# Constant matrix products in an attention stage's waits, a transposed layout for gate products, and weight remainders moved from GpSimd to VectorE

## The chip, the core and the metric

The kernel runs on one core of one Trainium2 chip. The metric is the device time of one execution in microseconds. The engines are TensorE (PE, with PEld for its weight loads), VectorE (DVE), ScalarE (ACT), GpSimd (POOL) and SyncE (SP), which here only issues DMAs.

## The reference

A linear attention without softmax feeds a mixture of experts in which each token goes to one expert.

```python
kv = einsum('bhsd,bhse->bhde', k, v)            # 8 batches, 8 heads, 576 tokens, 64 values
out = einsum('bhsd,bhde->bhse', q, kv)
out = out / sqrt(mean(out * out, -1) + 1e-6) * g_norm
x = out.transpose(0, 2, 1, 3).reshape(4608, 512)
e_idx = argmax(x @ w_gate, axis=1)              # 8 experts
gate_w = softmax(x @ w_gate)[token, e_idx]
eom = sigmoid(x @ w_output_gate)
for e in range(8):                              # w1[e]: 512 x 1024, w2[e]: 1024 x 512
    mask = e_idx == e
    y[mask] = gate_w[mask] * eom[mask, e] * (relu(x[mask] @ w1[e]) @ w2[e])
```

## The kernel before

**Attention stage (`p1_main`, to about 118 us).** For each batch, `kv_part` (line 469) multiplies k and v of five chunks of tokens (four of 128 and one of 64) into one PSUM tile, 64 x 64 per head, two heads side by side. `kvT_part` (494) transposes the result with two products against the identity. `m_part` (503) multiplies it by the gate weights (16 values per head: 8 logits and 8 output gates). Both results stand together in `augs`, so that `out_tile` (524) gets, with one product per pair of heads, the attention output of 128 tokens and every head's share of the gate products. The 36 output tiles of a batch are done while the next batch is worked on. ScalarE copies each tile out of PSUM in three steps: the rows (555), their squares (557), the gate products `gp` (558). `gp` has the layout token tile, head, 16 values.

**Routing.** The 36 tiles fall in four groups (10, 10, 4, 12). `route` (581) is a generator that `advance` moves on by a step after each tile. It works out the reciprocal norms (597 to 620, in `xtail`), scales `gp` by them (627; group 0 on GpSimd, the others on VectorE), sums over the heads (631, `lg`), takes the maximum and the expert's one-hot row (`ohb`), counts with products of `ones` (690), and places each token: `la` (717 to 731) is a one-hot matrix per tile, made by GpSimd, ScalarE or VectorE as the letters of `PLACES` say. After group 2 (24 tiles) the largest expert is known: the lead expert. Its first 384 rows are run 0, its other rows run 1 (3 tiles); runs 2 to 8 are the other experts.

**Precision.** Products run in fp32r with each operand split into a high and a low part: three products instead of one. `split` (199) makes the high part of a 128 x 1024 block of weights on one engine and the low part (weights minus high part) on another. `SPLITS` gives the engines for the lead expert: four blocks of first weights, then four of second weights. A `P` as second letter means GpSimd. Rows are scaled by their norms in `scale_heads` (245): on GpSimd ahead of time (`scale_rows`) or, with a `V` in `NORMS`, on VectorE when the tile is staged.

**Order.** In the attention stage the order on TensorE, ScalarE, VectorE and GpSimd is the order of the program, written by hand with `HOOKS` (steps after a given tile) and `TAIL` (steps after the last tile): `L` is the next step of the lead expert (`stage`, `split`, `mm1`), `S` the next split of its second weights, `R` one `advance`. In the expert part it is by hand for TensorE, ScalarE and VectorE. Between the two, a planner puts instructions that are ready into gaps; so the first nine products of `mm2` stand ahead of the sixth `mm1` step. Every engine runs its queue in order. Loads are issued by SyncE as memory slots come free.

**Buffers in PSUM.** `ps_b` (tag "big", 2 tiles) serves the output tiles, `m_part` and `mm1`; `ps_t` (tag "t", 2 tiles) serves `kv_part`, `kvT_part` and the row transposes of `stage`.

Of the kernel before, what the change touches and what calls it, by code (L numbers as in the profile page):

```python
# [11 lines left out]
F32 = mybir.dt.float32  # L12
# [5 lines left out]
ALU = mybir.AluOpType  # L18
AX = mybir.AxisListType
ET = mybir.EngineType  # L20

P = 128
B, H, S, D = 8, 8, 576, 64
NTOK = B * S
DM = H * D
E = 8
# [5 lines left out]
W = D + 2 * E  # L32
# [16 lines left out]
GMAX = max(GR)  # L49
# [28 lines left out]
APART = (2,)  # L78


SPLITS = ['VV', 'AV', 'AV', 'AV', 'AP', 'AP', 'AP', 'AP']
NORMS = ("PPP", "VPVP")
PLACES = ['P', 'P', 'PAV', 'PAV', 'PAV']

ROUND = 1.5 * 2.0 ** 30

# [49 lines left out]
def body(ctx: ExitStack, tc: tile.TileContext, kvm, rem, qT, wg, gn, w1, w2, kc, xs, tab, out):  # L136
    nc = tc.nc
# [27 lines left out]
    ps_t = main.enter_context(tc.tile_pool(name="ps_t", bufs=2, space=psum))  # L165
# [237 lines left out]
    sm = p1.enter_context(tc.tile_pool(name="sm", bufs=2))  # L403
# [7 lines left out]
    w = XW - DM  # L411
# [11 lines left out]
    ones = c1.tile([P, P], BF16, name="ones")  # L423
# [33 lines left out]
    def load(spare):  # L457

        while loads and len(free) > spare:
# [6 lines left out]
            nc.sync.dma_start(out=t[:n], in_=src)  # L466
            where[k] = t

    def kv_part(b):

        r = rt[b // 2]
        q0 = (b % 2) * 64
        ps = ps_t.tile([P, 512], F32, name="kvps", tag="t")
        for s in range(5):
            for p in range(NP):
                for u in range(2):
                    c = slice(p * P + u * D, p * P + (u + 1) * D)
                    if s < 4:
                        k, v = kvt[(b, s)][:, 0, c], kvt[(b, s)][:, 1, c]
                    else:  # L480
                        k, v = r[q0:q0 + 64, 0, c], r[q0:q0 + 64, 1, c]

                    nc.tensor.matmul(ps[u * D:(u + 1) * D, p * D:(p + 1) * D], k, v, start=(s == 0 and p == 0),  # L483
                                     stop=(s == 4 and p == NP - 1))
        for c in range(4):
            give(kvt.pop((b, c)))
        if b % 2:
            give(rt.pop(b // 2))
        nc.scalar.copy(augs[b % 3][:, :, 0:D], ps[:, 0:NP * D].rearrange("q (p d) -> q p d", p=NP))
        cp = wk.tile([P, NP * D], F32, name="kvc", bufs=1)  # L490
        nc.vector.tensor_copy(cp, ps[:, 0:NP * D])
        return cp

    def kvT_part(cp):

        ps = ps_t.tile([P, 2, P], F32, name="kvTps", tag="t")
        for i in range(2):
            nc.tensor.transpose(ps[:, i, :], cp[:, i * P:(i + 1) * P], ident)
        t = wk.tile([P, 2, P], F32, name="kvT", bufs=1)
        nc.scalar.copy(t, ps)  # L500
        return t

    def m_part(b, kvT):
        a = augs[b % 3]
        ps = ps_b.tile([P, 2, 512], F32, name="mps", tag="big")
        for i in range(2):
            for u in range(2):
                for w in range(2):
                    r = slice(w * D, (w + 1) * D)
                    nc.tensor.matmul(ps[u * D:(u + 1) * D, w, i * 16:i * 16 + 16], kvT[r, i, u * D:(u + 1) * D],  # L510
                                     gw[r, i, u * 16:u * 16 + 16], start=True, stop=True)
        nc.scalar.copy(a[:, :, D:D + 16].rearrange("q (i w) x -> q w i x", w=2),
                       ps[:, :, 0:32].rearrange("q w (i x) -> q w i x", i=2))
# [10 lines left out]
    def out_tile(g):  # L524
        gi, t, n = group_of(g)
        if t == 0:
            gst[gi] = (sm.tile([P, GMAX, E], F32, name="ss"),
                       sm.tile([P, GMAX, H, 16], F32, name="gp"),
                       sm.tile([P, GMAX, 16], F32, name="lg"))
        ss, gp, lg = gst[gi]  # L530
        if g in BIG:
            chunk[:] = [g, mem.tile([P, BIG[g], DM], F32, name="xrow", tag=f"xT{list(BIG).index(g)}")]
        elif not chunk:
            chunk[:] = [g, take([P, 2, DM], F32, "xrow")]
        xrow = chunk[1][:, g - chunk[0]]
        ps = ps_b.tile([P, 2, 512], F32, name="ops", tag="big")
        parts = []
        n0 = g * P
        while n0 < (g + 1) * P:
            b = n0 // S  # L540
            n1 = min((g + 1) * P, (b + 1) * S)
            parts.append((b, n0 - g * P, n1 - n0))
            n0 = n1
        for p in range(NP):
            for b, r0, m in parts:
                q0 = g % 2 * P + r0

                for u in range(2):
                    r = slice(u * D, (u + 1) * D)
                    nc.tensor.matmul(ps[r0:r0 + m, u, p * W:(p + 1) * W], qt[g // 2][r, p, q0:q0 + m],  # L550
                                     augs[b % 3][r, p, :], start=True, stop=True)
        if g % 2:
            give(qt.pop(g // 2))
        v = ps[:, :, 0:NP * W].rearrange("q u (p x) -> q u p x", p=NP)
        nc.scalar.copy(xrow.rearrange("q (p u d) -> q u p d", p=NP, u=2), v[:, :, :, 0:D])  # L555
        sq = wk.tile([P, H, D], F32, name="sq", bufs=4)
        nc.scalar.activation(sq.rearrange("q (p u) d -> q u p d", u=2), v[:, :, :, 0:D], AF.Square)  # L557
        nc.scalar.copy(gp[:, t].rearrange("q (p u) x -> q u p x", u=2), v[:, :, :, D:W])  # L558
        squares.append((sq, ss[:, t, :], gi if t + 1 == n else None))
        c0, x = chunk  # L560
        k = x.shape[1]
        if g + 1 == c0 + k:
            xwrite(c0, xs[1 + c0 * P:1 + (c0 + k) * P, 0:DM].rearrange("(t p) x -> p t x", p=P), x)
            chunk.clear()
# [16 lines left out]
    def route(gi):  # L581
# [4 lines left out]
        ss, gp, lg = gst[gi]  # L586
        n = len(GROUPS[gi])
        last = gi + 1 == len(GROUPS)
        g0 = GROUPS[gi][0]
        vec = nc.vector  # L590
# [13 lines left out]
        u = sm.tile([P, GMAX, E], F32, name="ru")[:, :n]  # L604
        rv = xtail[:, g0:g0 + n, C_RMS - DM:C_RMS - DM + H]

        q = 0.375 ** 0.5
# [14 lines left out]
        gpv = gp[:, :n]  # L622
        halves = [slice(0, E), slice(E, 2 * E)] if gi in APART else [slice(0, 2 * E)]

        def scaled(j, eng):
            w = j.stop - j.start
            eng.tensor_tensor(out=gpv[:, :, :, j], in0=gpv[:, :, :, j],
                              in1=rv.unsqueeze(3).to_broadcast([P, n, E, w]), op=ALU.mult)

        def summed(j):  # L630
            vec.tensor_reduce(out=lg[:, :n, j], in_=gpv[:, :, :, j].rearrange("p t h j -> p t j h"), axis=AX.X, op=ALU.add)

        scaled(halves[0], veng(gi))
        if gi in APART:
# [211 lines left out]
    def p1_main():  # L846
        load(SPARE)
        for b in range(B):
            lim = tiles_ready(b - 1) if b else 0
            cp = kv_part(b)  # L850
            load(SPARE)
            run_out(lim)
            kvT = kvT_part(cp)
            run_out(lim)
            run_out(lim)
            m_part(b, kvT)
            while done_tiles < lim:
                run_out(lim)
        while done_tiles < NT:
            run_out(NT)  # L860
        for step in TAIL:
            act(step)
        while routing:
            advance()

    vec = nc.vector
# [315 lines left out]
```

## Time and profile before

| | |
|---|---|
| median of 3 runs (604.76, 607.0, 602.8 us) | 604.76 us |
| the profiled execution's own time | 609.39 us |
| span of the profile | 607.4 us |
| mean granted clock of TensorE | 0.934 |
| TensorE busy | 557.5 us (92%), 4179 products |
| VectorE, ScalarE, GpSimd busy | 262.4, 221.0, 163.4 us |

The span runs from the first to the last instruction; the 2 us beside it are start and end. "Granted clock" is the share of TensorE's full clock of 2.4 GHz that it was given; 0.50 is 1.2 GHz. In the 40 slices of the page the clock is below full in the first ten (some 152 us) and full from there on, apart from the end. TensorE is busy 90% or more of nearly every slice after the eleventh.

### The profile page before, as it was taken

What the parts mean: (1) busy time and instruction counts of PE and PEld (TensorE: products, weight loads), DVE (VectorE), ACT (ScalarE), POOL (GpSimd) and SP (SyncE); (2) the same over time, 40 slices, a digit from 0 to 9 for tenths busy, and PEclk for the clock granted to TensorE, in tenths of its full rate; (3) what the DMA queues carried; (4) which work ended last, traced back from release to release, by engine and by line L of the source; (5) the groups of instructions that cost most, each with busy time, mean ns of one, the idle gap of its engine ahead of it and who ended that gap; (6) DMA issues with size and microseconds to landing.
All of it is one profiled execution on the core that took longest, in us unless ns stands there. A gap on an engine that the chain in (4) does not pass through costs nothing.

```text
span 607.4 us, 10470 instructions
## 1 busy us (share of the span) xinstructions
PE 557.5 (92%) x4179; PEld 497.3 (82%) x4179; DVE 262.4 (43%) x546; ACT 221.0 (36%) x413; POOL 163.4 (27%) x163
## 2 busy tenths in 40 slices
PE   3889879858999999999999999999999999999991
PEld 3678868747788899889988987998799889889880
DVE  1123588789614556415440443235235325424300
ACT  0425564644224435323432343234234423523310
POOL 2001044542860620540063027104500630110010
PEclk9957786578999999999999999999999999999997
DMA  8999993590563622442334333524432452110010
GB/s 271 364 408 409 404 375 85 168 373 2 141 242 122 210 91 73 138 171 72 103 119 155 104 105 98 169 70 141 139 120 70 138 183 71 53 53 2 4 49 10
DMA packets 33459, 92.24 MB, mean 152 GB/s; under 512 B 8801, under 2 KB 8929, under 8 KB 33408
## 3 DMA queue, kind: packets, MB, share of 16 engines
q1 hardware_dynamic: 26672, 71.63, 33.4%
q0 software_dynamic: 6304, 19.70, 10.3%
q8 instruction: 34, 0.56, 0.4%
q10 hardware_dynamic: 432, 0.21, 0.1%
q14 instruction: 17, 0.14, 0.1%
HBM read 72.34 MB, written 19.70 MB: 152 GB/s over the span
## 4 chain that ended last, share of the span: by engine, by line
PE 63%; issue 17%; DMA 7%; DVE 6%; ACT 3%; POOL 2%; SPq 0%; POOLq 0%; DVEq 0%
PE yps L359 26%; PE hps L310 25%; PE ops L550 4%; PE kvps L483 3%; PE tps L272 3%; DMA ld<-rem 2%; DMA ld<-qT 2%; PE yps L353 2%; POOL out L370 2%; DMA ld<-kvm 2%; ACT xrow L555 1%; ACT sq L557 1%; DMA wraw<-w 1%; DMA xg<-xs,gidx 1%; DVE ss L571 1%
## 5 line engine op out<-in xcount | busy, mean ns | idle before, releaser
L310 PE MATMUL hps<-xT,whi 128*128 128x256 f32 (+8 forms) x1024 | 192.3, 306 | 9.2 <-DVE hT L326 8.1
L359 PE MATMUL yps<-whi,hT 128*128 128x512 f32 (+3 forms) x592 | 194.9, 397 | 0.0
L310 PEld LDWEIGHTS hps<-xT,whi 128*128 128x128 f32 x1024 | 159.4, 191 | 11.8 <-DVE hT L326 8.8
L359 PEld LDWEIGHTS yps<-whi,hT 128*128 128x128 f32 (+3 forms) x592 | 110.1, 186 | 24.1
L310 PE MATMUL hps<-xT,wlo 128*128 128x304 f32 (+8 forms) x512 | 119.2, 304 | 0.0
L359 PE MATMUL yps<-wlo,hT 128*128 128x512 f32 (+3 forms) x296 | 115.9, 392 | 0.0
L326 DVE SCALAR_TENSOR_TENSOR hT<-hps,hT 128x512 fp32r<-128x512 f32 (+6 forms) x112 | 57.9, 518 | 124.2 <-ACT hT L325 124.2
L325 ACT ACTIVATE hT<-hps 128x512 fp32r<-128x512 f32 (+6 forms) x112 | 51.6, 461 | 151.8 <-PE hps L310 118.8
L310 PEld LDWEIGHTS hps<-xT,wlo 128*128 128x128 f32 x512 | 87.0, 190 | 0.0
L370 POOL DMA_INDIRECT out<-y,oidx x42 | 44.8, 1068 | 154.2 <-ACT y L369 109.5
L240 POOL DMA_INDIRECT xg<-xs,gidx x42 | 42.4, 1010 | 138.1 <-PE tps L272 92.1
L359 PEld LDWEIGHTS yps<-wlo,hT 128*128 128x128 f32 (+3 forms) x296 | 55.1, 186 | 11.2
L218 DVE SCALAR_TENSOR_TENSOR wlo<-wraw,gcol,whi 128x1024 fp32r<-128x1024 f32 x32 | 44.6, 1394 | 40.3 <-ACT whi L215 40.3
L550 PE MATMUL ops<-aug,ld 64*128 64x80 f32 (+1 forms) x640 | 49.2, 328 | 5.9 <-ACT gp L558 5.6
L248 POOL TENSOR_TENSOR xg<-xg 128x512 f32<-128x512 f32 (+7 forms) x40 | 44.3, 1110 | 31.9 <-DMA xg<-xs,gidx 31.6
L550 PEld LDWEIGHTS ops<-aug,ld 64*128 64x128 f32 (+1 forms) x640 | 44.8, 231 | 8.8 <-ACT gp L558 6.4
L369 ACT ACTIVATE y<-yps,tl 128x512 f32<-128x512 f32 (+3 forms) x37 | 25.5, 689 | 71.7 <-PE yps L359 68.6
L277 ACT CAST xT<-tps 128x512 fp32r<-128x512 f32 (+9 forms) x45 | 23.2, 519 | 68.0 <-PE tps L272 66.2
L483 PE MATMUL kvps<-ld 128*64 128x64 f32 (+1 forms) x640 | 36.4, 298 | 11.8 <-DMA ld<-kvm 10.9
L278 DVE TENSOR_TENSOR xT<-tps,xT 128x512 fp32r<-128x512 f32 (+9 forms) x45 | 27.2, 605 | 45.4 <-ACT xT L277 44.9
L483 PEld LDWEIGHTS kvps<-ld 128*64 128x64 f32 (+1 forms) x640 | 32.9, 207 | 14.9 <-DMA ld<-kvm 12.5
L225 DVE TENSOR_TENSOR wlo<-wraw,whi 128x1024 fp32r<-128x1024 f32 x28 | 34.3, 1225 | 14.1 <-ACT whi L222 8.7
(159 smaller groups left out, 403.7 us busy)
## 6 DMA issues: line engine op xcount, KB each, us to landing
wraw<-w SPq DMA_DIRECT2D x64, 512.0 KB, 3.3
ld<-kvm SPq DMA_DIRECT2D x32, 512.0 KB, 10.2
ld<-qT SPq DMA_DIRECT2D x18, 512.0 KB, 10.2
xs<-xrow SPq DMA_DIRECT2D x13, 512.0 KB, 10.3
xs<-xrow SPq DMA_DIRECT2D x2, 1280.0 KB, 13.7
ld<-rem SPq DMA_DIRECT2D x3, 512.0 KB, 11.0
xg<-xs,gidx POOLq DMA_INDIRECT x42
out<-y,oidx POOLq DMA_INDIRECT x42
```

The source lines that it names most:

```text
L218: eng.scalar_tensor_tensor(out=lo, in0=r, scalar=gcol[:, 0:1], in1=hi.bitcast(F32), op0=ALU.mult, op1=ALU.subtract)
L225: eng.tensor_tensor(out=lo, in0=r, in1=hi.bitcast(F32), op=ALU.subtract)
L240: nc.gpsimd.indirect_dma_start(out=x[:M, :], out_offset=None, in_=rows, in_offset=bass.IndirectOffsetOnAxis(ap=gidx[:M, p, t:t + 1], axis=0))
L248: eng.tensor_tensor(out=v, in0=v, in1=f, op=ALU.mult)
L278: nc.vector.tensor_tensor(out=lo[:, :, c0:c0 + M], in0=v, in1=hi.bitcast(F32)[:, :, c0:c0 + M], op=ALU.subtract)
L310: nc.tensor.matmul(ps[:, j, :n], w[:, o:o + P], x[d][:, j * N:j * N + n], start=(d == 0 and k == 0), stop=(d == 3 and k == 2))
L325: nc.scalar.activation(hh, x, AF.Relu)
L326: nc.vector.scalar_tensor_tensor(out=v(h[:, l:l + n]), in0=x, scalar=0.0, in1=hh.bitcast(F32), op0=ALU.max, op1=ALU.subtract)
L359: nc.tensor.matmul(ps[:M], a, b, start=(f == 0 and k == 0), stop=(f == 7 and k == 2))
L370: i_ = nc.gpsimd.indirect_dma_start(out=out, out_offset=bass.IndirectOffsetOnAxis(ap=oidx[:M, p, t:t + 1], axis=0), in_=y[:M], in_offset=N ...
L483: nc.tensor.matmul(ps[u * D:(u + 1) * D, p * D:(p + 1) * D], k, v, start=(s == 0 and p == 0), stop=(s == 4 and p == NP - 1))
L550: nc.tensor.matmul(ps[r0:r0 + m, u, p * W:(p + 1) * W], qt[g // 2][r, p, q0:q0 + m], augs[b % 3][r, p, :], start=True, stop=True)
```

## The change

Four edits. Constant products: `constant` multiplies the 128 x 128 matrix `ones` (bf16) by a view of itself that is 128, 256 or 512 columns wide; the results are not read. They stand ahead of each kv chunk of 128 tokens in batches 0 to 2, ahead of the transposes in `kvT_part`, ahead of the products of `m_part`, and (512 columns, in a `ps_t` tile of their own) behind them. The gate products `gp` get the heads innermost. The four second weights of the lead expert get their low parts on VectorE instead of GpSimd, and one tile of run 1 is scaled there (`NORMS`; the fourth letter has no tile). In the last group, `la` is made on VectorE where it was on GpSimd (`PLACES`, 4 of 12 tiles).

```diff
-SPLITS = ['VV', 'AV', 'AV', 'AV', 'AP', 'AP', 'AP', 'AP']
-NORMS = ("PPP", "VPVP")
-PLACES = ['P', 'P', 'PAV', 'PAV', 'PAV']
+SPLITS = ['VV', 'AV', 'AV', 'AV', 'AV', 'AV', 'AV', 'AV']
+NORMS = ("PPP", "VVVV")
+PLACES = ['P', 'P', 'PAV', 'VAV']
+COLD_B = 3
+COLD = (2, 20, 2, 3, 3)
...
+    def constant(ps, n, start=True):
+        for _ in range(n):
+            k = ps.shape[1] // P
+            nc.tensor.matmul(ps, ones, ones.unsqueeze(1).to_broadcast([P, k, P]), start=start, stop=start)
...  kv_part
         for s in range(5):
+            if s < 4 and b < COLD_B:
+                constant(ps[:, 256:512], COLD[0] + (COLD[1] if b == 0 and s == 0 else 0), s == 0)
...  kvT_part
-        ps = ps_t.tile([P, 2, P], F32, name="kvTps", tag="t")
+        ps = ps_t.tile([P, 512], F32, name="kvTps", tag="t")
+        constant(ps[:, 256:512], COLD[2])
+        ps = ps[:, 0:256].rearrange("q (i x) -> q i x", i=2)
...  m_part
         ps = ps_b.tile([P, 2, 512], F32, name="mps", tag="big")
+        constant(ps[:, 1, 256:512], COLD[3])
...  out_tile
-                       sm.tile([P, GMAX, H, 16], F32, name="gp"),
+                       sm.tile([P, GMAX, 16, H], F32, name="gp"),
...
-        nc.scalar.copy(gp[:, t].rearrange("q (p u) x -> q u p x", u=2), v[:, :, :, D:W])
+        nc.scalar.copy(gp[:, t].rearrange("q x (p u) -> q u p x", u=2), v[:, :, :, D:W])
...  route
-            eng.tensor_tensor(out=gpv[:, :, :, j], in0=gpv[:, :, :, j],
-                              in1=rv.unsqueeze(3).to_broadcast([P, n, E, w]), op=ALU.mult)
+            eng.tensor_tensor(out=gpv[:, :, j], in0=gpv[:, :, j],
+                              in1=rv.unsqueeze(2).to_broadcast([P, n, w, E]), op=ALU.mult)
...
-            vec.tensor_reduce(out=lg[:, :n, j], in_=gpv[:, :, :, j].rearrange("p t h j -> p t j h"), axis=AX.X, op=ALU.add)
+            vec.tensor_reduce(out=lg[:, :n, j], in_=gpv[:, :, j], axis=AX.X, op=ALU.add)
...  p1_main
             m_part(b, kvT)
+            constant(ps_t.tile([P, 512], F32, name="cps", tag="t"), COLD[4])
```

## Rows read from the trace of the kernel before

**Rows 1.** The page's chain that ended last, by engine:
```profile
PE 63%; issue 17%; DMA 7%; DVE 6%; ACT 3%; POOL 2%; SPq 0%; POOLq 0%; DVEq 0%
```
**Rows 2.** Windows: length, busy PE, PEld, DVE, ACT, POOL, then clock, DMA share, GB/s.
```profile
36.80:49.30 12.50, 11.71 (x156) 10.81 (x150) 3.76 (x6) 6.98 (x18) 0.00 (x0) 0.50 1.03 410
56.50:59.50 3.00, 3.00 (x50) 2.86 (x50) 0.80 (x2) 1.24 (x3) 2.37 (x1) 0.50 1.03 408
66.80:73.30 6.50, 6.50 (x100) 6.27 (x98) 2.86 (x12) 2.49 (x6) 0.00 (x0) 0.50 1.02 406
80.30:83.50 3.20, 3.20 (x58) 3.06 (x58) 2.81 (x12) 1.24 (x3) 3.20 (x7) 0.50 1.09 390
90.60:100.50 9.90, 8.76 (x131) 8.38 (x132) 9.17 (x41) 2.97 (x9) 5.10 (x8) 0.50 0.45 133
159.30:594.00 434.70, 434.70 (x2555) 387.17 (x2555) 168.04 (x289) 151.38 (x241) 119.78 (x114) 1.00 0.33 110
```
**Rows 3.** TensorE's waits, 36.8 to 159.3 us: total, times, longest.
```profile
PE hps L310 <- DVE hT L326: 8.1, 2, 7.5
PE ops L550 <- ACT gp L558: 4.9, 5, 1.7
PE rps L690 <- DVE ohb L657: 4.3, 2, 3.3
```
**Rows 4.** TensorE's instructions in order: start, length, instruction, count.
```profile
38.44 3.71 PE L550 MATMUL ops<-aug,ld 64*128 64x80 f32 x32
...
47.13 3.75 PE L483 MATMUL kvps<-ld 128*64 128x64 f32 x80
...
52.23 2.16 PE L550 MATMUL ops<-aug,ld 64*128 64x80 f32 x32
...
96.49 4.53 PE L483 MATMUL kvps<-ld 128*64 128x64 f32 x80
```
**Rows 5.** VectorE's instructions in order, 84 to 155 us.
```profile
86.03 1.48 DVE L627 TENSOR_TENSOR gp<-gp,xtail 128x1280 f32<-128x1280 f32 x1
87.54 2.30 DVE L631 TENSOR_REDUCE lg<-gp 128x160 f32<-128x1280 f32 x1
...
108.45 0.28 DVE L728 TENSOR_SCALAR la<-ni,rlon 128x128 bf16<-128x128 f32 x1
...
126.82 2.32 DVE L601 TENSOR_SCALAR ry<-ra 128x96 int32<-128x96 int32 x1
...
129.46 0.26 DVE L610 TENSOR_TENSOR ru<-ru,ra 128x96 f32<-128x96 f32 x1
...
138.60 2.81 DVE L631 TENSOR_REDUCE lg<-gp 128x192 f32<-128x1536 f32 x1
...
151.64 1.96 DVE L894 SCALAR_TENSOR_TENSOR tbl<-tb 128x48 f32<-128x48 f32 x1
```
**Rows 6.** Line 225: durations in ns (min/median/max), first and last start.
```profile
L225 DVE TENSOR_TENSOR wlo<-wraw,whi x28: 1224/1226/1227, 216.6 to 571.4; 128x1024 fp32r<-128x1024 f32 x28
...
L225 POOL TENSOR_TENSOR wlo<-wraw,whi x4: 2350/2388/2393, 126.7 to 151.1; 128x1024 fp32r<-128x1024 f32 x4
```
**Rows 7.** Tile gp, ScalarE's copies, in the same columns.
```profile
L558 ACT COPY gp<-ops x36: 266/272/314, 24.9 to 119.6; 128x128 f32<-128x128 f32 x36
```
**Rows 8.** The chain that ended last, 154 to 160 us: start, length, work.
```profile
154.69 3.77 DMA xg<-xs,gidx
```
**Rows 9.** The same chain, two runs of wide products.
```profile
137.55 4.22 PE hps L310 x12
...
189.13 2.08 PE yps L359 x9
```
**Rows 10.** SyncE's load issues in order; then kv loads: KB each, median us to landing.
```profile
27.75 5.71 SPq L466 DMA_DIRECT2D ld<-kvm  x4
...
63.83 5.85 SPq L466 DMA_DIRECT2D ld<-kvm  x4
...
ld<-kvm SPq DMA_DIRECT2D x32, 512.0 KB, 10.2
```

## The prediction

> **What bounds the kernel now.** I first read the page's chain of work that ended last. TensorE holds 63% of it, VectorE and ScalarE 9%, and "issue" 17% [rows 1]. So the next view is TensorE's stretches with the clock that it was granted [rows 2]. From 159.3 to 594.0 us it is busy for the whole 434.7 us at full clock (1.00 is 2.4 GHz): nothing that the change touches lies there, and what reaches TensorE earlier at 159.3 us ends the kernel as much earlier. The change has to earn its time before that, in the attention stage and in the lead expert's first product. There the clock alternates. Five stretches between 36.8 and 100.5 us were granted 0.50 (1.2 GHz), 35.1 us in all, with 33.2 us of work in them. Each fall came after the products of output tiles and the small products of `m_part`, with waits between them; each rise came in a run of kv products. The waits of TensorE [rows 3] are the third view: 8.1 us for hT from VectorE, 7.5 us of it in one place; 4.9 us in 5 places for ScalarE's copy of gp; 4.3 us for ohb from VectorE, 3.3 us of it in one place.
>
> **The lead expert.** The 7.5 us for hT arise in VectorE's queue. It holds three operations of 96 columns that took about 2.3 us each instead of 0.26 us, and later one of 48 columns with 1.96 us [rows 5]. Each lies over a subtraction of a second weight's low part on GpSimd, four in all of about 2.39 us [rows 6]. The change takes these four from GpSimd. Saved on VectorE: 3 x 2.04 + 1.75 = 7.9 us. Added on VectorE: the four subtractions, 1.226 us each in 28 like cases [rows 6], with overlap 1.19 us, 4.8 us; and four more `la` at 0.28 us [rows 5], 1.1 us. The last reduction of gp (2.81 us for 1536 columns) now reads neighbours. The nearest row is the product over gp, 1.48 us for 1280 columns, against 2.30 us for the reduction of the same 1280 [rows 5]; scaled, 1.75 us, saved 1.1 us. Bounds for that: nothing, and 1.1 us. The sum is 4.8 + 1.1 - 7.9 - 1.1 = -3.1 us. VectorE's queue runs nearly without a break from there into the gather of the second run's rows (3.77 us) and the transposes after it [rows 8], so I count all of it. What is late next is the same queue: the first hT comes about 4.9 us earlier, the second only about 3.6 us, since the subtractions stand ahead of it. The one row scaling that goes to VectorE waits there for its gathered rows; behind it are only that tile's copy and subtraction, and TensorE has products of an earlier tile meanwhile, so zero; without that cover it costs its own 0.7 us. No DMA is added; GpSimd's gathers come behind less work.
>
> **The gate products.** The second group's reduction stands on the path: the 3.3 us wait for ohb [rows 3] ends behind a product of 1.48 and a reduction of 2.30 us [rows 5]. Saved 0.8 us. The price is in ScalarE: its copy of gp, 272 ns, 36 times [rows 7], now writes with a step of 8 values. No row shows such a write. Bounds: nothing, and the ratio of reduction to product (2.30/1.48), 0.15 us each. I take nothing, since the rows show the cost only where a step is read; the other end is a rival below.
>
> The Trainium skill (SBUF — State Buffer, section "Door 1: The DMA port swizzle") says that an access that leaves its 16-byte line pays, so four float32 is the widest free step. The reduction of gp with a step of 16 values agrees (2.30 against 1.48 us [rows 5]); by that rule the penalty goes from VectorE's reductions to ScalarE's copies, and the time would be the third rival's.
>
> **The constant products.** Per batch there are five of 256 columns and three of 512; batches 0 to 2 get eight more in the kv stage and batch 0 another 20. No row shows one. Nearest: 9 products of 512 columns in 2.08 us at full clock, 0.23 us each; 12 of 384 columns in 4.22 us, at half clock, 0.35 us each [rows 9]. Scaled by columns, a batch pays 5 x 0.12 + 3 x 0.23 = 1.3 us at full clock and 5 x 0.23 + 3 x 0.47 = 2.6 us at half. The first 22 lie in front of the first load and cost nothing; the extra ones of batches 1 and 2 lie where TensorE waits for loads. The three of 512 use a tile of their own and fill the wait for gp behind `m_part` (4.9 us in 5 places [rows 3]), 0.7 us a batch. The three ahead of `m_part` write into the tile that `m_part` itself waits for, so they stand behind that wait and fill little. About 0.5 us a batch stays open, 3.1 us over the six batches that end after 36.8 us.
>
> What they can give: two tiles' products take 3.71 us at half clock and 2.16 us at full, a ratio of 0.58 [rows 4]. The 33.2 us of work in the five slow stretches [rows 2] would shrink by at most 0.42 x 33.2 = 13.9 us. About 15 us of that are kv products (a batch 4.53 us at half clock [rows 4]), short ones that I expect to shrink by a quarter only: 2.5 us less. The first stretch is held by loads: the fourth batch's last kv load was issued by 33.5 us and landed by about 43.7 us (with 10.2 us from issue to landing [rows 10]), and its products began at 47.1 us [rows 4], so it can begin 3.4 us earlier and not 4.9: 1.5 us less. Minus the 3.1 us, full success is -6.8 us. I take -5.6 us, as a stretch or two will still fall, above all at the wait for ohb. Later loads don't forbid it: the last batch's kv loads were issued by 69.7 us [rows 10], and its products began at 96.49 us [rows 4]. The bounds are -6.8 us and, with the clock as it is and nothing filled, 8 x 2.6 = +20.8 us.
>
> **Sum.** -3.1 - 0.8 - 5.6 = -9.5 us. The profiled execution took 609.39 us, 4.6 us above the median of the runs, 604.76 us; against its own time the sum is 599.9 us. Taken from the median, the forecast is 595 us.
>
> **Rivals.**
> 1. The clock is not held. From 66.8 to 73.3 us TensorE was busy for all 6.50 us and was granted 0.50 [rows 2], so more busy time alone need not lift it. Then only VectorE's 3.9 us remain, less about 1 us of constants that nothing hides: 602 us. Against it: these products use the whole array, and stand in the stretches after which the clock fell. The Trainium skill (TensorE: Matmul & The Clock Gate, section "What's actually happening") has the clock set by how busy TensorE has been; the busy column of that stretch disagrees, and by that rule constants add nothing where there is no wait.
> 2. Slower. In TensorE's ordered queue the constants stand ahead of the transposes and of `m_part`. At half clock a batch pays 2.6 us and hides about 1.0 us behind `m_part`; six batches make +9.6 us, minus VectorE's 3.9 us: 610.5 us. It decides if the stretches from 36.8 to 100.5 us stay at 0.50 for as long as now. Against it: the waits that are there to be filled, 4.9 us for gp [rows 3].
> 3. ScalarE pays for the step. Some 20 of the 36 copies lie where TensorE waits for gp or ScalarE paces the last tiles: 20 x 0.15 = 3 us, 598 us.
> 4. The change does nothing at the clock because loads set the pace. The last batch's loads lie too far ahead of their use for that [rows 4, 10]; I count it with the first rival.
>
> **How the numbers follow.** Forecast 0.52 (own range 591 to 599 us), rivals 1 and 4 0.25, rival 2 0.12, rival 3 0.11. The low end, 589.5 us, takes full success at the clock, less work at half clock in the lead expert, and 2 us for the runs' spread (602.8 to 607.0 us); the high end, 602.5 us, takes in the third rival and most of the first. 1% is 6 us, about what a measurement here can tell from no change. Faster than 598.7 us: nearly all of the forecast, half of rival 3 and little of rival 1, 0.56. Slower than 610.8 us: half of rival 2, 0.07. Within: 0.37.
>
> **What would show it.** No VectorE operation of 96 columns over 0.4 us in the lead expert, and a longest wait for hT near 2.6 us; the reduction of 1280 columns near 1.5 us; gp's copy still near 272 ns; the clock above 0.9 for most of 36 to 95 us; the last batch's kv products beginning near 90 us instead of 96.5; no wait of TensorE from its second run on. I am wrong if those kv products begin no earlier, if one hT still waits over 5 us, or if copies of gp take 0.4 us.

## The result and the profile after

| kernel | median | its runs | ratio to the kernel before |
|---|---|---|---|
| before | 603.78 us | 602.76 to 607.0 (4) | |
| changed | 596.79 us | 596.37 to 597.85 (4) | 0.9878 [0.9835, 0.9921] |

The change makes the kernel 7.0 us faster (1.2%); the forecast was 595 us and -9.5 us. The profiled execution of the kernel before (609.39 us) is one of its longest and that of the changed kernel (597.85 us) stands 1.1 us above its median, so the two profiles lie further apart than the medians; sizes below come from stages and from ratios. The kernel before differs from run to run in how long TensorE is held at half clock: its 56 runs beside the experiments have a mean granted clock of 0.932 to 0.956, those with 0.934 or less take 606.49 to 609.67 us and those with 0.953 or more 602.84 to 603.97 us, while the changed kernel's ten runs (four here, six as a0) have 0.960 to 0.966.

The chain of work that ended last, by engine (it answers to [rows 1]): VectorE and ScalarE fall from 9% to 6%, TensorE rises from 63% to 65%.

```profile
PE 65%; issue 17%; DMA 7%; DVE 4%; POOL 2%; ACT 2%; SPq 1%; POOLq 0%; DVEq 0%
```

Windows by granted clock, with the columns of [rows 2]: length, busy PE, PEld, DVE, ACT, POOL, then clock, DMA share, GB/s.

```profile
36.80:80.50 43.70, 40.05 (x800) 33.89 (x799) 26.52 (x69) 28.42 (x74) 9.43 (x11) 1.00 1.03 405
81.20:90.80 9.60, 8.84 (x103) 7.07 (x104) 6.89 (x33) 4.47 (x12) 5.17 (x9) 0.50 1.04 366
104.90:118.20 13.30, 10.77 (x55) 9.34 (x54) 8.94 (x20) 7.76 (x17) 5.87 (x6) 0.50 0.88 288
129.10:135.00 5.90, 5.14 (x16) 5.14 (x17) 5.66 (x21) 2.00 (x6) 0.00 (x0) 0.50 0.00 1
147.50:583.00 435.50, 435.20 (x2555) 387.23 (x2555) 167.44 (x288) 151.49 (x241) 117.81 (x113) 1.00 0.34 110
```

Where the work of the first four slow stretches of [rows 2] is done, the clock is now full for 43.7 us. It still falls three times, at 81, 105 and 129 us; the last row is the part that the change doesn't touch, as long as before for the same 2555 products.

TensorE's waits from 36.8 us to the second run's first transposes, as in [rows 3] (total, times, longest):

```profile
PE rps L705 <- DVE ohb L672: 5.4, 2, 3.0
PE hps L314 <- DVE hT L330: 4.4, 3, 2.5
PE mps L477 <- ACT gp L573: 2.1, 4, 0.6
PE tps L276 <- POOL xg L252: 1.0, 1, 1.0
PE ops L565 <- ACT gp L573: 0.7, 2, 0.5
```

The 7.5 us for hT became 2.5. The wait for gp ahead of the output tiles shrank from 4.9 us to 0.7. Ahead of `m_part` it was 1.5 us before and is 2.1 now; the constants there stand behind the wait, as predicted. The wait for ohb did not shrink in sum: 4.3 before, 5.4 now. Its second-group part did, from 3.25 to 2.47 us, and the last group's, in the lead expert, grew from 1.05 to 2.95. And there is a new wait for rows of the lead expert that GpSimd has gathered and scaled.

TensorE in order of time, as in [rows 4]: start, length, instruction, count.

```profile
42.57 2.70 PE L495 MATMUL kvps<-ld 128*64 128x64 f32 x80
...
81.97 0.54 PE L705 MATMUL rps<-ohb,ones 128*128 128x80 bf16 x10 [2.47 <-DVE ohb L672]
...
82.41 0.84 PE L477 MATMUL mps<-ones 128*128 128x256 bf16 x3
...
83.73 1.46 PE L477 MATMUL cps<-ones 128*128 128x512 bf16 x3
85.12 3.71 PE L565 MATMUL ops<-aug,ld 64*128 64x80 f32 x32
88.76 3.71 PE L495 MATMUL kvps<-ld 128*64 128x64 f32 x80
...
109.09 1.12 PE L276 MATMUL tps<-ident,xg 128*128 128x128 f32 x4 [1.05 <-POOL xg L252]
...
147.44 0.66 PE L276 MATMUL tps<-ident,xg 128*128 128x128 f32 x4 [0.59 <-DVE tl L272]
```

The fourth batch's kv products begin 4.6 us earlier than in [rows 4], the last batch's 7.7 us earlier. The clock falls at 80.8 us, inside the 2.47 us wait for ohb (79.5 to 82.0 us).

VectorE in order, as in [rows 5], and ScalarE's copies of gp in the columns of [rows 7] (ns, min/median/max):

```profile
77.07 1.48 DVE L642 TENSOR_TENSOR gp<-gp,xtail 128x1280 f32<-128x1280 f32 x1
78.59 1.49 DVE L646 TENSOR_REDUCE lg<-gp 128x160 f32<-128x1280 f32 x1
...
117.10 0.21 DVE L616 TENSOR_SCALAR ry<-ra 128x96 int32<-128x96 int32 x1
...
117.64 0.26 DVE L625 TENSOR_TENSOR ru<-ru,ra 128x96 f32<-128x96 f32 x1
...
125.01 1.74 DVE L646 TENSOR_REDUCE lg<-gp 128x192 f32<-128x1536 f32 x1
...
139.50 0.26 DVE L915 TENSOR_TENSOR t<-tblps,perm 128x96 f32<-128x96 f32 x1 [2.08 <-PE tblps L773]
...
142.13 0.20 DVE L910 SCALAR_TENSOR_TENSOR tbl<-tb 128x48 f32<-128x48 f32 x1
```

```profile
L573 ACT COPY gp<-ops x36: 389/399/426, 25.4 to 109.1; 128x128 f32<-128x128 f32 x36
```

No operation of 96 columns stalls any more, the reductions cost what the products cost, and each copy of gp takes 127 ns longer (36 copies, one for each output tile of the kernel; a batch has four and a half tiles).

### The profile page after: what moved, and what is told of

It is laid out like the page before. It is cut to its first block, busy times and chain, and to the rows that moved or that the text cites. A ratio compares the mean times of both kernels' runs of the same rounds, so it can differ in the third digit from the quotient of the medians.

```text
span 596.0 us, 10672 instructions
## 1 busy us (share of the span) xinstructions
PE 558.9 (94%) x4287; PEld 488.6 (82%) x4287; DVE 255.3 (43%) x555; ACT 223.7 (38%) x413; POOL 149.4 (25%) x154
## 4 chain that ended last, share of the span: by engine, by line
PE 65%; issue 17%; DMA 7%; DVE 4%; POOL 2%; ACT 2%; SPq 1%; POOLq 0%; DVEq 0%
PE yps L363 27%; PE hps L314 27%; PE kvps L495 3%; PE tps L276 2%; PE ops L565 2%; DMA ld<-qT 2%; PE yps L357 2%; POOL out L374 2%; DMA ld<-rem 2%; DMA ld<-kvm 2%; DMA wraw<-w 1%; PE cps L477 1%; DVE ss L586 1%; POOL xg L244 1%; DVE lg L646 1%
## 5 line engine op out<-in xcount | busy, mean ns | idle before, releaser
L252 POOL TENSOR_TENSOR xg<-xg 128x512 f32<-128x512 f32 (+7 forms) x39 | 41.6, 1069 | 33.9 <-DMA xg<-xs,gidx 32.9
L229 DVE TENSOR_TENSOR wlo<-wraw,whi 128x1024 fp32r<-128x1024 f32 x32 | 39.2, 1224 | 14.1 <-ACT whi L226 7.1
L565 PEld LDWEIGHTS ops<-aug,ld 64*128 64x128 f32 (+1 forms) x640 | 36.4, 190 | 7.3 <-ACT aug L527 3.2
L565 PE MATMUL ops<-aug,ld 64*128 64x80 f32 (+1 forms) x640 | 40.5, 283 | 1.7 <-ACT gp L573 0.7
L219 ACT ACTIVATE whi<-wraw,gcol 128x1024 fp32r<-128x1024 f32 x31 | 35.5, 1144 | 0.0
L226 ACT CAST whi<-wraw 128x1024 fp32r<-128x1024 f32 x32 | 33.2, 1040 | 1.4 <-DMA wraw<-w 1.4
## 6 DMA issues: line engine op xcount, KB each, us to landing
ld<-kvm SPq DMA_DIRECT2D x32, 512.0 KB, 10.1
```

The costliest lines, as they stand in the source:

```text
L219: he.activation(hi, r, AF.Copy, scale=gcol[:, 0:1])
L226: he.copy(hi, r)
L229: eng.tensor_tensor(out=lo, in0=r, in1=hi.bitcast(F32), op=ALU.subtract)
L252: eng.tensor_tensor(out=v, in0=v, in1=f, op=ALU.mult)
```

## The experiments

Each kernel was compared with the kernel before on the same chip. e1 to e4 share one chip, a0 to e8 another, e9, e11 and e14 a third, and e12 ran on a fourth. Ratios from different chips compare only roughly: of the runs of the kernel before, 14 of 23 had a clock of 0.934 or less beside e1 to e4, and 2 of 11 beside a0 to e8.

| kernel | median | before there | ratio |
|---|---|---|---|
| e1_constants | 600.34 | 607.25 | 0.9889 [0.9864, 0.9915] |
| e2_engines | 605.4 | 607.25 | 0.9969 [0.9944, 0.9993] |
| e3_layout | 606.38 | 607.25 | 0.9986 [0.9958, 1.0014] |
| e4_quarter_array | 598.31 | 607.25 | 0.9859 [0.9834, 0.9884] |
| a0_changed | 597.69 | 605.38 | 0.9884 [0.9858, 0.9910] |
| e5_heads_outer | 597.41 | 605.38 | 0.9881 [0.9854, 0.9908] |
| e7_order | 595.45 | 605.38 | 0.9845 [0.9818, 0.9872] |
| e8_order_constants | 594.9 | 605.38 | 0.9841 [0.9815, 0.9868] |
| e9_no_front | 599.29 | 606.93 | 0.9883 [0.9855, 0.9911] |
| e11_ohb_both | 599.21 | 606.93 | 0.9870 [0.9839, 0.9901] |
| e14_no_kv | 604.08 | 606.93 | 0.9899 [0.9847, 0.9951] |
| e12_combined | 594.12 | 606.73 | 0.9798 [0.9768, 0.9828] |

**One part of the change at a time (e1, e2, e3).** e1 is the kernel before with the constants alone:

```diff
+COLD_B = 3
+COLD = (2, 20, 2, 3, 3)
...  and the calls of constant in kv_part, kvT_part, m_part, p1_main
```

> The kernel before with the constant products alone. My theory (the clock gives most): 598 to 601 us, that is 3 to 6 us less; the clock at 1.00 from about 19 to past 80 us; the last batch's kv products begin near 90 us; the longest wait for hT still near 7.5 us. Rival (the gain came from VectorE's queue alone): 603 to 605 us, no change, even though the clock shows as held.

e2 is the kernel before with the engines alone:

```diff
-SPLITS = ['VV', 'AV', 'AV', 'AV', 'AP', 'AP', 'AP', 'AP']
-NORMS = ("PPP", "VPVP")
-PLACES = ['P', 'P', 'PAV', 'PAV', 'PAV']
+SPLITS = ['VV', 'AV', 'AV', 'AV', 'AV', 'AV', 'AV', 'AV']
+NORMS = ("PPP", "VVVV")
+PLACES = ['P', 'P', 'PAV', 'VAV']
```

> The kernel before with the moves from GpSimd to VectorE alone (SPLITS, NORMS, PLACES). My theory: 2 us less (602 us), the longest wait for hT near 3 us, the clock of the attention stage as before. Rival (VectorE's queue gave all): 597 to 598 us. Second rival (what the queue gains is given back at the next wait): no change.

e3 is the kernel before with the layout of gp alone:

```diff
-sm.tile([P, GMAX, H, 16], F32, name="gp")
+sm.tile([P, GMAX, 16, H], F32, name="gp")
...  and its views in out_tile and route
```

> The kernel before with the layout of gp alone, heads innermost. The changed profile has the reductions at 1.48 and 1.74 us (saved 0.8 and 1.1 us) and ScalarE's copies at 399 instead of 272 ns (0.127 us x 36 = 4.6 us more). My theory: the two cancel, within 1 us of the kernel before. Rival (the copies stand where TensorE waits for ScalarE): 2 to 4 us slower. Rival (the reductions are the path): 2 us faster.

By the ratios, with 607.25 us: constants -6.7 us (5.2 to 8.3), engines -1.9 us (0.4 to 3.4), layout -0.9 us (between -2.6 and +0.9). So the constants are most of the change, and the engines' part is real but small. Among runs with the same clock (0.932 to 0.934) the medians say the same of the small parts: -2.0 us for the engines, -0.7 for the layout. The constants' figure is one over the mix of runs: e1's median lies 8.1 us below the runs of the kernel before with that clock, and 2.8 us below the three with 0.950 or more. TensorE's waits in e1, from 36.8 us on, show a place where the gain can be lost again:

```profile
PE hps L314 <- DVE hT L330: 8.0, 2, 7.4
PE rps L705 <- DVE ohb L672: 4.2, 2, 3.2
PE tps L276 <- POOL xg L252: 3.9, 2, 2.8
```

TensorE comes to the lead expert early and waits 3.9 us for its rows, in two places: these follow the third group's routing on VectorE, a write to memory, a gather and a scaling on GpSimd, and constants on TensorE don't hurry any of them. In e2, the hT wait is short and the ohb wait is the longer one:

```profile
PE rps L690 <- DVE ohb L657: 7.5, 2, 4.0
...
PE hps L310 <- DVE hT L326: 4.0, 3, 2.3
```

**The constants on a quarter of the array's columns (e4).** The changed kernel, its constants with 32 columns of weights instead of 128:

```diff
-nc.tensor.matmul(ps, ones, ...)
+nc.tensor.matmul(ps[0:32], ones[:, 0:32], ...)
```

> The changed kernel with constant products of the same number and the same columns, but only 32 of the 128 columns of the array (weights 128 x 32, results in 32 partitions). If the clock answers to the time that TensorE is busy: 597 us and the same granted clock as the changed kernel. If it answers to how much of the array works, as I think: the clock falls several times between 20 and 80 us, and the time is 600 to 604 us.

A window of e4 with the columns above, and its constants of 256 columns (ns, min/median/max):

```profile
36.80:80.50 43.70, 40.17 (x798) 33.46 (x797) 26.34 (x68) 28.39 (x74) 9.20 (x11) 1.00 1.03 405
```

```profile
L477 PE MATMUL mps<-ones x24: 269/270/421, 15.4 to 98.5; 128*32 128x256 bf16 x24
```

The granted clock of this window is 1.00 as well, and the time is no worse. My reason that "these products use the whole array" falls: with 32 of its columns the clock held too. (All 128 rows were still fed; fewer rows were not tried.)

**The layout undone in the changed kernel (a0, e5).** a0 is the changed kernel again, for the same chip; e5 has gp's old layout:

```diff
-sm.tile([P, GMAX, 16, H], F32, name="gp")
+sm.tile([P, GMAX, H, 16], F32, name="gp")
...  and its views
```

> The changed kernel itself, on the same chip as the three below, as their reference. Both theories: 0.985 to 0.990 of the kernel before.

> The changed kernel with the old layout of gp (heads outside), everything else as changed. Theory A (in the changed kernel the layout costs about what it saves: ScalarE's copies 36 x 0.127 us delay the attention stage, the reduction saves 1.1 us in the lead expert): last batch's kv products about 1.7 us earlier, the lead expert about 1 us longer, time within 1 us of the changed kernel. Theory B (the layout helps, as my sum has it): 1 to 2 us slower than the changed kernel.

No difference (597.69 and 597.41 us). Tile gp in e5:

```profile
L573 ACT COPY gp<-ops x36: 267/272/309, 24.2 to 106.1; 128x128 f32<-128x128 f32 x36
L646 DVE TENSOR_REDUCE lg<-gp x5: 566/2307/2722, 55.4 to 124.3; 128x160 f32<-128x1280 f32 x2, 128x32 f32<-128x256 f32 x2, 128x192 f32<-128x1536 f32 x1
```

The layout buys 0.8 us in a reduction and pays 36 x 0.127 = 4.6 us of ScalarE for it. Where that reaches TensorE: the fourth batch's kv products begin at 40.72 and 41.04 us in the kernels with constants and the old layout (e5, e1), at 41.50 to 42.57 us in the eight with constants ahead of the kv chunks and the new one. By the last batch nothing of it is left to see (87.31 and 87.09 us against 85.37 to 88.94). In the lead expert the layout earns: from its first transposes to run 1's it takes 39.94 us in e5, 38.11 in a0.

**The order in the lead expert (e7, e8).** e7 is the changed kernel with two of the splits of second weights moved behind the lead steps that followed them; e8 adds constants to the last group's wait for ohb:

```diff
-TAIL = "QLLLLRRRSLSRRSLLRRRLSLRRSRLSLL"
+TAIL = "QLLLLRRRLSSRRLLSRRRLSLRRSRLSLL"
```

```diff
...  e8, route, ahead of the counting products
+        if last:
+            constant(ps_t.tile([P, 512], F32, name="lps", tag="t"), 12)
```

> The changed kernel with another order by hand in TAIL: the second weights' splits (S) come behind the first products (L) instead of in front of them, so that hT stands ahead of a subtraction of 1.2 us in VectorE's queue. If the subtractions now on VectorE are what delays TensorE in the lead expert: the two waits for hT shrink by 1.1 us each, and the time falls by 1 to 2 us. If the table that follows VectorE's whole queue sets the end: the waits shrink and the time stays.

> As e7, and 12 constant products of 512 columns in the lead expert, where TensorE waits 3 us for the last group's ohb. If the fall of the clock at 128.5 us (24 products of the lead expert in 7.0 us instead of 4.2) makes TensorE late for the tables (VectorE waits 2.1 us for them): the clock holds from 118 us on and the time is another 1.5 to 2.5 us below e7. Rival (VectorE's queue ends last there anyway): no difference to e7.

TensorE's waits in e7:

```profile
PE rps L705 <- DVE ohb L672: 6.6, 2, 4.1
PE tps L276 <- POOL xg L252: 2.4, 1, 2.4
PE mps L477 <- ACT gp L573: 2.1, 4, 0.6
PE hps L314 <- DVE hT L330: 2.0, 2, 1.1
```

hT falls from 4.4 to 2.0 us and ohb rises from 5.4 to 6.6. The median falls by 2.2 us against a0; the two intervals overlap, but the trace agrees: VectorE no longer waits for the tables, and the lead expert, from its first transposes to run 1's, takes 36.31 us instead of 38.11. So part of what the moved subtractions cost was their place in the queue. e8, a window:

```profile
118.50:152.00 33.50, 28.75 (x165) 23.57 (x164) 27.77 (x78) 13.50 (x26) 8.91 (x9) 1.00 0.50 167
```

In e8 the clock is full where it fell at 126.1 us in a0, 128.6 in the changed kernel's profile and near 128.6 in e7, and the time moves by 0.5 us only, less than the intervals can tell: VectorE is what TensorE waits for there, and its queue takes as long at either clock (from the second block's low part at 114.82 us to 142.34 us without a wait of 0.2 us or more in e8, 115.26 to 142.92 in e7).

**Which constants hold the clock (e9, e11, e14).**

```diff
 e9:  COLD = (2, 20, 0, 0, 3)
 e14: COLD = (0, 0, 2, 3, 3)
...  e11, e8 with, in route
+        if last or gi == 1:
+            constant(ps_t.tile([P, 512], F32, name="lps", tag="t"), 12 if last else 9)
```

> The changed kernel without the constants of 256 columns ahead of the transposes of kv and ahead of the products of m_part (five a batch). Theory A (the prediction's): they stand behind the wait for the tile they write into, so they fill little and hold nothing; the clock stays at 1.00 from 20 to 80 us as in the changed kernel, the last batch's kv products begin at 87 to 89 us, the time is 597 us, within 1 us. Theory B: they are part of what holds the clock; without them it falls to 0.50 somewhere between 30 and 80 us, the last kv products begin at 91 us or later, the time is 600 us or more. Theory C: they are pure cost, 5 x 0.1 us in each of 8 batches; the last kv products begin 2 to 3 us earlier.

> The kernel of e8_order_constants with 9 more constant products of 512 columns in the second group's wait for ohb, ahead of the counting products at 78 to 81 us, after which the clock fell in every run so far. Theory A (TensorE's own work sets when the lead expert begins): the clock holds through 80 to 91 us, the last kv products take 2.7 us instead of 4.1 and the lead expert's first transposes come 2 us earlier: 592.5 to 593.5 us. Theory B (the third group's routing and its gather set it, as the wait for the gathered rows says): the clock holds, but the wait of the first transposes for the gathered rows grows from 2.4 to about 4.5 us, and the time is 594.5 to 595.5 us, as in e8_order_constants.

> The changed kernel without the constants ahead of the kv chunks of batches 0 to 2. Theory A (the prediction's: the first batches wait for loads): the clock is at 0.50 for some stretch before 40 us, but the fourth batch's kv products begin within 1 us of the changed kernel's 42.6 us, and the time is 597 us, within 1 us. Theory B: the clock falls at 29 us as before the change and stays down into the fourth batch; the kv products of batches 3 and 7 begin 2 to 4 us later than in the changed kernel, and the time is 599 to 600 us.

e9: the clock holds from 20 to 78 us and the last kv products begin at 86.33 us, 2.4 us earlier than in the changed kernel's profile (0.4 earlier than in a0's). So in this execution the clock holds to 78 us without the five products ahead of the transposes and of `m_part`. They do cost something, as theory C has it: from the fourth batch's kv products to the seventh's it is 28.3 us in e9 and 29.8 in a0. Most of this is given back behind the second group's ohb, where TensorE now waits for ScalarE's copy into `augs`:

```profile
82.70 3.70 PE L565 MATMUL ops<-aug,ld 64*128 64x80 f32 x32 [1.35 <-ACT aug L527]
```

Two of e9's six runs have a mean clock of 0.949, below all ten of the changed kernel, so it is not shown that the clock holds without the five in every run. e14, TensorE and a window:

```profile
47.19 4.03 PE L495 MATMUL kvps<-ld 128*64 128x64 f32 x80
```

```profile
33.50:49.75 16.25, 15.93 (x192) 13.28 (x191) 3.76 (x6) 7.62 (x18) 0.00 (x0) 0.50 1.03 408
```

Without the constants in the first batches the clock falls at 33 us and the fourth batch begins where it did before the change [rows 4]: theory B by the trace. But its runs are of two kinds, 596.23 and 597.51 us with a clock of 0.969 and 0.968, and four from 603.98 us on with 0.958 or less. In the first two the clock can hardly have fallen like this; it seems that these constants hold it in some runs and aren't needed in others. e11, windows:

```profile
81.20:90.80 9.60, 8.67 (x170) 6.90 (x168) 9.01 (x44) 5.94 (x16) 5.54 (x8) 1.00 1.03 354
91.80:121.80 30.00, 27.52 (x211) 23.53 (x212) 20.68 (x63) 16.26 (x39) 7.71 (x10) 0.50 0.71 234
```

The clock holds over the second group's wait, as wished, and the last kv products begin at 85.37 us. Then TensorE meets the `la` matrices, which come one by one from GpSimd (5 waits, 1.7 us); the clock falls there and stays down for 30 us, and the lead expert begins at 111.08 us, later than the 109.09 us of the changed kernel. Neither theory had that.

The three profiled executions are also spoilt by something that none of the theories named; what the other executions did there isn't seen. Here are e9's instructions of four engines in order of time, where run 1's tiles are scaled and staged, and then a0's at the same place:

```profile
144.18 0.69 DVE L252 TENSOR_TENSOR xg<-xg 128x512 f32<-128x512 f32 x1 [0.86 <-DMA xg<-xs,gidx]
...
146.56 0.59 ACT L281 CAST xT<-tps 128x512 fp32r<-128x512 f32 x1 [1.74 <-PE tps L276]
...
147.79 2.07 DVE L252 TENSOR_TENSOR xg<-xg 128x512 f32<-128x512 f32 x1
...
148.24 1.06 POOL L252 TENSOR_TENSOR xg<-xg 128x512 f32<-128x512 f32 x1
...
149.91 1.12 PE L276 MATMUL tps<-ident,xg 128*128 128x128 f32 x4 [2.25 <-DVE xg L252]
```

```profile
145.77 0.59 ACT L281 CAST xT<-tps 128x512 fp32r<-128x512 f32 x1 [0.73 <-PE tps L276]
...
147.00 0.68 DVE L252 TENSOR_TENSOR xg<-xg 128x512 f32<-128x512 f32 x1
...
149.37 1.04 POOL L252 TENSOR_TENSOR xg<-xg 128x512 f32<-128x512 f32 x1 [0.87 <-DMA xg<-xs,gidx]
```

In e9 VectorE scales the second tile 2.07 us long, over a scaling of GpSimd; TensorE waits 2.25 us, the clock is at 0.50 from 149.7 to 153.1 us, and from the second run's first transposes to the end it is 452.3 us instead of 448.2 in a0. e11 and e14 show the same scaling (2.03 and 2.04 us), and 452.3 and 450.6 us to the end; in e14 the clock did not fall there. In a0 GpSimd's scaling begins after VectorE's has ended.

**Three edits together (e12).**

```diff
-TAIL = "QLLLLRRRSLSRRSLLRRRLSLRRSRLSLL"
-NORMS = ("PPP", "VVVV")
-COLD = (2, 20, 2, 3, 3)
+TAIL = "QLLLLRRRLSSRRLLSRRRLSLRRSRLSLL"
+NORMS = ("PPP", "VPVP")
+COLD = (2, 20, 0, 0, 3)
```

> The changed kernel with three edits: the order of e7_order, no constants ahead of the transposes of kv and of m_part (as in e9_no_front), and the letters VPVP in NORMS as before the change, so that GpSimd scales the second tile of the second run in its own queue and VectorE does not meet GpSimd there. In the profiles of e9, e11 and e14 VectorE's scaling of that tile took 2.0 to 2.1 us instead of 0.68, over a scaling of GpSimd, TensorE waited 2.25 us for it and its clock fell. Theory A (that meeting is the cause): TensorE waits under 1 us from the second run's first transposes on, some 448.3 us from there to the end of the span, no VectorE scaling of 128 rows over 0.8 us, the clock at 1.00 there; with e7's order and some 1 us less of constants the ratio to the kernel before is 0.981 to 0.984, 593.5 to 595.5 us where that kernel takes 605. Theory B (ScalarE's copy of the transposed rows, 0.9 us late in those three profiles, is the cause by itself): a wait of 2 us or more stays at the second tile, 450 us or more to the end, ratio 0.987 or more.

594.12 us, ratio 0.9798: faster than the kernel before. It is faster than the changed kernel too: its interval doesn't meet that of 0.9884, and its six runs (591.98 to 595.25 us) lie below the changed kernel's ten (595.13 to 598.05), with one overlap. A gain over e7 (594.63 to 596.21 us, on another chip) isn't shown, nor which of the three edits carries the rest. Run 1's tiles in e12, and all of TensorE's waits after 140 us:

```profile
142.95 0.69 DVE L252 TENSOR_TENSOR xg<-xg 128x512 f32<-128x512 f32 x1 [0.74 <-DMA xg<-xs,gidx]
144.66 1.04 POOL L252 TENSOR_TENSOR xg<-xg 128x512 f32<-128x512 f32 x1 [0.22 <-DMA xg<-xs,gidx]
...
148.20 1.58 DVE L252 TENSOR_TENSOR xg<-xg 52x512 f32<-52x512 f32 x1
```

```profile
PE tps L276 <- DVE tl L272: 0.5, 1, 0.5
```

From the second run's first transposes (143.70 us) to the end it is 448.2 us, as theory A says. VectorE still meets GpSimd at the third tile, of 52 rows, which takes it 1.58 us instead of the 0.68 in a0; TensorE doesn't wait for that. But ScalarE's copy was on time in this execution, so e12 shows the good course and not what the new letters do when that copy is late: theory B is not excluded by it.

## Why the prediction was right, and where it was not

**Engines: right.** Without the reduction, my lead expert term is 4.8 + 1.1 - 7.9 = -2.0 us; e2 measured -1.9. The stalls went (0.20 to 0.26 us for every such operation of 96 columns) and the longest wait for hT came out at 2.5 us against the 2.6 expected. In the changed kernel the lead expert, from its first transposes to run 1's, takes 38.35 us (109.09 to 147.44) instead of 40.7: -2.4 where the whole term, reduction included, said -3.1. The step that was too good is "I count all of it": VectorE's queue is no longer without a break, it waits 2.08 us for the tables from TensorE, and with the subtractions ahead of ohb TensorE's wait for it grew (1.05 to 2.95 us in the lead expert). e7 shows that the place can be chosen better: there VectorE's wait is gone and the lead expert takes 36.31 us, 4.4 less than before.

The Trainium skill (SBUF — State Buffer, section "SBUF: two separate sides") has VectorE and GpSimd share a pair of ports under an exclusive lock: of a GpSimd operation and a VectorE operation of the kinds that it lists (two inputs in SBUF are one of them), whichever starts first keeps it for its whole instruction and the other blocks. The stalls of [rows 5] under the subtractions of [rows 6], and their end here, agree. e9 differs in a detail: VectorE's operation has the earlier recorded start (147.79 against 148.24 us), and is the one that takes three times its length.

**The row scaling on VectorE: zero, but not safe.** In the changed kernel's profiles it costs nothing, as said. "Without that cover it costs its own 0.7 us" was too little: where GpSimd scales at the same time, TensorE waited 2.25 us, and run 1 and what follows took 4.1 us longer to the end, some of it at half clock (e9 against a0).

**Gate products: the gain as said, the price mis-sized.** The reduction went from 2.30 to 1.49 us, as predicted. "I take nothing" for ScalarE's stepped write failed: it costs 127 ns a copy, close to the upper bound of 0.15 us that I had set and left to the third rival, and the text had named 0.4 us a copy as a sign of being wrong. Measured, the layout is worth nothing (e5) to -0.9 us (e3, interval across zero), where the reductions were to bring 0.8 + 1.1 us. Rival 3's mechanism is there; its 3 us were too much. Of the 4.6 us that the copies take longer, between 0.5 and 1.9 us reach the fourth batch and none is seen at the last; that the rest lies beside other work is argued, not shown.

The Trainium skill (SBUF — State Buffer, section "Door 1: The DMA port swizzle") puts the penalty on a step beyond four float32. Both sides agree here: the reduction is freed of it (2.30 to 1.49 us), the copy that now writes with a step of eight values pays it (272 to 399 ns).

**Constants and clock: right, and somewhat too small.** -5.6 us predicted, -6.7 in e1, at full success of -6.8. That the sizes meet so closely is in part luck. The term was read from an execution of 609.39 us with a clock of 0.934, one of the longest, and was taken off the median; against such runs e1 gains 8.1 us and against the shortest 2.8. The term also left out what lies behind 100.5 us, where the clock is at 0.50 for 27 us before and 20 us after, and the first of its stretches began at 29.0 us, of which [rows 2] show the part from 36.8. Of 35.1 us at 0.50 between 36.8 and 100.5 us some 10 are left, and the fall that stayed is the one at the wait for ohb, as said. Their own price was near the one taken: at half clock three of 256 columns took 0.84 us and three of 512 took 1.46 (the rows at 82.41 and 83.73 us above), 0.28 and 0.49 us each, against 0.23 and 0.47. Two sizes were off in the change's favour. The kv products shrank from 3.75 us, partly at full clock already, to 2.70 us where the clock is full, by 28% and more, not by a quarter. And the fourth batch began 4.6 us earlier, where I allowed 3.4 for its loads: these were issued earlier too, the last by 32.3 us instead of 33.5. e14 puts a limit on my remark that the first batches wait for loads: their constants fill those waits, but without them, in its profiled execution, the clock fell at 33 us and stayed down into the fourth batch. That the three ahead of `m_part` "fill little" fits e9, which drops them and the two ahead of the transposes and gains 1.5 us over three batches. That the use of the whole array is a reason for the clock to hold fell with e4.

**The sum.** The parts alone give -6.7 - 1.9 - 0.9 = -9.5 us, the forecast's figure; together they gave -7.0 (and 0.9884, -7.0, in a0). A loss of 2.5 us in the sum is not shown by that: the parts were measured on a chip where the kernel before took 607.25 us, and e4 there, all four edits with narrower constants, gives -8.6 us (7.0 to 10.1). The traces do have a place where something is given back: between the attention stage and the lead expert, TensorE now waits for gathered rows (at the first transposes 1.05 us in the profile after, 2.4 in a0 and e7, 2.8 in e1, none before). The prediction did not name that wait as late next.

**Rivals.** Rival 1 (clock not held) and rival 2 (constants as pure cost) did not come: the clock is at 1.00 for the 43.7 us in which they needed it at 0.50. Rival 4 (loads set the pace) did not come either: in the changed kernel the kv products of the fourth batch follow the output tiles without a wait. The range was 589.5 to 602.5 us, and all four runs lie within.

## What to carry to other kernels

Products that compute nothing can pay where TensorE's clock falls behind short waits: put them into the wait, ahead of real work that is bound by TensorE, and not where another engine sets the end (e8). Look at the clock of every run, and not only at the profiled one: one profile shows one of several courses. When a layout frees one engine of a step, look for the engine that now has it, and price that from the freed one's own rows, not at zero. Where two engines hinder each other, a meeting that one profile doesn't show can be what another run pays for; work that stands on one queue can't meet itself.

## What the runs showed of the hardware that was not expected

- The same program takes different courses at the clock. Beside e1 the kernel before ran at 0.933 or 0.934 in 14 of 23 runs (607.11 to 609.67 us) and at 0.945 to 0.956 in the others (603.11 to 606.99 us).
- A stretch that is kept at full clock can be followed by a longer slow one: in e11 30 us at 0.50 with 27.52 us of work in them, behind 5 waits of at most 0.4 us, where the changed kernel had two stretches of 9.6 and 13.3 us.
- In the profiles of e9, e11 and e14, ScalarE began the copy of transposed rows about 0.9 us late (1.63 to 1.68 us after the transposes began, against 0.70 in a0), with nothing in the trace that it waited for. VectorE's scaling stands behind that copy. Also, GpSimd's scaling began there right behind its gathers, where in a0 it first waited 0.87 us for its rows. The two together made the scalings meet. Its cause stays open: all three were profiled on one chip.
- The product over gp on GpSimd went from 2.37 us (e1, e5) to 2.91 us with the heads innermost, though VectorE's took 1.48 us either way:

```profile
L642 POOL TENSOR_TENSOR gp<-gp,xtail x1: 2913/2913/2913, 51.9 to 51.9; 128x1280 f32<-128x1280 f32 x1
```
